# Three rows of a modulation matrix by DMA transpose and VectorE product-sums, and half of the row statistics on ScalarE

## The chip, the cores and the metric

The kernel runs on one core of a Trainium2 chip. The metric is the device time in microseconds (us) of one execution. Each kernel was executed several times, and the kernel before again beside each; a ratio is the mean time of one kernel's runs over that of the other's runs of the same rounds. The runs came in four jobs; each job had its own runs of the kernel before. The profile is one execution, whose span (first to last instruction) is about 2 us shorter than the reported time.

## The reference

```python
mod = (silu(c) @ w_mod).reshape(1, 6, 1, -1)         # c: 1 x 1024, w_mod: 1024 x 6144
sa, ca, ga, sb, cb, gb = ...                          # six rows of 1024
h = layernorm(x) * (1 + ca) + sa                      # x: 2048 x 1024
x = x + ga * linear_attention(h, wqkv) @ wo           # 32 heads of 32, phi(t) = elu-like
h = layernorm(x) * (1 + cb) + sb
x = x + gb * (silu(h @ w_gate) * (h @ w_up)) @ w_down # width 3584
```

Nearly all work is dense matmuls. The six rows of `mod` are 0.02% of its operations, but the kernel makes them in pieces on TensorE and VectorE, and this is what the change is about. `sa` and `ca` are needed at once and stay as they are; `ga`, `cb`, `sb` ("late rows") are needed from 129 us on, `gb` from about 380 us on.

## The kernel before

Tokens go in four chunks of 512 (four tiles of 128). A stage multiplies a chunk by one weight: K, V and Q stages have eight groups of eight matmuls, 128x128 by 128x512, into one PSUM bank; five banks rotate. The program issues each engine's instructions in a fixed order; `put(label, f)` places `f` behind the group of that label. So ("V", 1, 3) is the fourth V group of chunk 1. The late rows were made in two ways.

CB on TensorE, as one-column matmuls:

```python
def late_vec(q, kb, slot):                    # twice, 32 matmuls each
    for ii in range(NB // P):
        for j in range(DC):
            nc.tensor.matmul(bank[7][:, col:col + 1], lhsT=wml[slot][:, j, ii * P:(ii + 1) * P],
                             rhs=scT[:, j:j + 1], start=False, stop=(j == DC - 1), ...)
```

GA, SB (and GB) as partial sums on VectorE, eight multiply-adds for each half row, split into a high and a low bf16 part, and summed over the partitions by TensorE, either with an all-ones stationary operand (which also copies the row into all partitions) or into columns:

```python
def late_sum(acc, kb, slot, js):
    for j in js:                              # first one a plain multiplication
        nc.vector.scalar_tensor_tensor(out=dst, in0=wml[slot][:, j, :], scalar=scF[:, j:j + 1], in1=dst, ...)
def late_bc(kb, hl, dst):                     # GA and GB: 2 matmuls of 512 columns for a half row
    for s_ in range(2):
        nc.tensor.matmul(b[:], lhsT=ones[:], rhs=hl[:, s_, :], ...)
def late_cols(q, kb, hl):                     # SB: 8 one-column matmuls for a half row
    ...
```

Row statistics of the normalization (`ln_stats`: two `bn_stats`, one `bn_aggr`, on VectorE) feed GpSimd, which writes the normalized tile, and a DMA transpose on the SP queue puts it into place. A later VectorE instruction modulates it; the K stage of that chunk needs it.

## Time and profile before

| | kernel before |
|---|---|
| time, median of the first 4 runs | 842.47 us (842.31 to 842.87) |
| span of the profiled execution | 840.4 us |
| TensorE waits in it | 3.7 us, all before 27 us |
| VectorE busy in the V stages of chunks 1, 2, 3 | 13.3, 12.9, 13.5 of 14 us |
| TensorE time of the late rows GA, CB, SB | 2.89 us |

The lines behind this stand in the prediction. In the page, a digit of a slice row is the busy share of one fortieth of the span in tenths. In a timeline line the first two numbers are start and duration; TensorE's matmuls overlap (the eight transposes at 7.69 us last 0.62, and the next group starts at 8.15), so what a group costs is the distance to the next group's start.

### The profile page before, as it was taken

The page shows a single profiled execution, that of the slowest core. Times are in us where ns is not written, and L with a number is a line of the kernel's source. Part 1 is how long each engine was busy: PE and PEld are TensorE (multiplying, and loading weights), DVE is VectorE, ACT ScalarE, POOL GpSimd, SP SyncE. Part 2 cuts the span into 40 slices and gives each one's busy share as a digit, 9 for nine tenths or more (in the row PEclk, how much of TensorE's full clock was granted, in tenths as well). Part 3 has the DMA queues.
Part 4 walks back from the last instruction along what each step waited for, and adds up shares of the span by engine and source line. Part 5 has one row for each costly group of instructions (what it writes and reads, how often), then busy time and mean ns, then how long its engine had stood idle before and what let it go on. Part 6 is the DMA issues. An engine that isn't in the chain of part 4 may idle for free.

```text
span 840.4 us, 10723 instructions
## 1 busy us (share of the span) xinstructions
PE 833.5 (99%) x4292; PEld 391.3 (47%) x4292; DVE 356.5 (42%) x668; ACT 145.1 (17%) x271; POOL 79.9 (10%) x143
## 2 busy tenths in 40 slices
PE   8999999999999999999999999999999999999998
PEld 4454444544444444444444444444444444444445
DVE  5768779988655656635341111111101211111111
ACT  4333333323211111111110001111000111100000
POOL 2124220022122323100000000000000000000000
PEclk9999999999999999999999999999999999999999
DMA  9985491056599899787874225555322555211210
GB/s 291 310 244 138 133 243 46 16 154 133 126 225 225 224 226 287 190 248 226 251 241 142 76 69 151 151 151 152 105 75 82 156 155 152 76 38 44 76 69 26
DMA packets 203905, 128.62 MB, mean 153 GB/s; under 512 B 50768, under 2 KB 190032, under 8 KB 203856
## 3 DMA queue, kind: packets, MB, share of 16 engines
q1 hardware_dynamic: 163008, 98.58, 41.1%
q10 hardware_dynamic: 38544, 20.98, 11.4%
q0 software_dynamic: 2304, 8.39, 2.6%
q8 instruction: 33, 0.54, 0.3%
q14 instruction: 16, 0.13, 0.1%
HBM read 103.81 MB, written 12.58 MB: 139 GB/s over the span
## 4 chain that ended last, share of the span: by engine, by line
PE 97%; SPq 1%; DMA 1%; issue 0%; DVE 0%
PE bank L553 23%; PE bank L534 23%; PE bank L528 23%; PE bank L272 7%; PE bank L485 7%; PE bank L264 7%; PE bank L249 6%; DMA M<-in_w_mod_dram 1%; PE bank L458 1%; PE bank L281 1%; SPq L148 1%; SPq L145 0%; PE bank L342 0%; SPq L140 0%; PE bank L328 0%; PE bank L364 0%
## 5 line engine op out<-in xcount | busy, mean ns | idle before, releaser
L534 PE MATMUL bank<-M,M 128*128 128x512 bf16 x896 | 211.7, 379 | 0.0
L528 PE MATMUL bank<-M,M 128*128 128x512 bf16 x896 | 211.6, 379 | 0.0
L536 DVE TENSOR_TENSOR M<-bank,e 128x512 bf16<-128x512 f32 x112 | 77.5, 692 | 248.5 <-PE bank L534 247.1
L553 PE MATMUL bank<-M,M 128*128 128x512 bf16 (+2 forms) x728 | 148.0, 363 | 0.0
L531 ACT ACTIVATE e<-bank 128x512 f32<-128x512 f32 x112 | 66.8, 597 | 436.3 <-PE bank L528 423.6
L553 PEld LDWEIGHTS <-M 128*128 128x128 bf16 x952 | 90.9, 98 | 103.0
L534 PEld LDWEIGHTS <-M 128*128 128x128 bf16 x896 | 87.7, 98 | 105.7
L528 PEld LDWEIGHTS <-M 128*128 128x128 bf16 x896 | 87.3, 98 | 103.9
L556 DVE TENSOR_TENSOR M<-bank,M 128x512 bf16<-128x512 f32 (+2 forms) x34 | 22.5, 661 | 169.9 <-PE bank L553 169.9
L249 PE MATMUL bank<-M,M 128*128 128x512 bf16 x256 | 57.9, 379 | 1.0 <-DVE M L231 0.6
L485 PE MATMUL bank<-M,M 128*128 128x512 bf16 x256 | 57.9, 379 | 0.0
L272 PE MATMUL bank<-M,M 128*128 128x512 bf16 x256 | 57.7, 379 | 0.0
L264 PE MATMUL bank<-M,M 128*128 128x512 bf16 x256 | 55.9, 379 | 0.0
L244 ACT ACTIVATE e<-bank 128x512 f32<-128x512 f32 x64 | 37.8, 598 | 100.5 <-PE bank L272 48.8
L553 PE MATMUL bank<-M 128*128 128x512 bf16 x224 | 51.0, 379 | 0.0
L246 DVE SCALAR_TENSOR_TENSOR M<-bank,e 128x512 bf16<-128x512 f32 x64 | 44.3, 692 | 3.9
L264 PEld LDWEIGHTS <-M 128*128 128x128 bf16 x256 | 25.0, 98 | 30.2
L485 PEld LDWEIGHTS <-M 128*128 128x128 bf16 x256 | 25.0, 98 | 29.7
L249 PEld LDWEIGHTS <-M 128*128 128x128 bf16 x256 | 24.2, 98 | 29.5 <-DVE M L231 2.1
L245 DVE TENSOR_SCALAR e<-e 128x512 f32<-128x512 f32 x64 | 27.7, 433 | 23.4 <-ACT e L244 23.4
L272 PEld LDWEIGHTS <-M 128*128 128x128 bf16 x256 | 24.5, 98 | 27.6
L487 DVE TENSOR_TENSOR M<-bank,M 128x512 f32<-128x512 f32 x32 | 22.0, 689 | 13.3 <-PE bank L485 13.1
(74 smaller groups left out, 362.4 us busy)
## 6 DMA issues: line engine op xcount, KB each, us to landing
M<-in_B_w_gate_dram SPq DMA_DIRECT2D x56, 512.0 KB, 3.9
M<-in_B_w_up_dram SPq DMA_DIRECT2D x56, 512.0 KB, 4.9
M<-in_w_mod_dram SPq DMA_DIRECT2D x8, 1024.0 KB, 8.7
x_scratch<-M POOLq DMA_DIRECT2D x16, 512.0 KB, 5.6
M<-x_scratch ACTq DMA_DIRECT2D x16, 512.0 KB, 3.4
M<-in_B_w_down_dram SPq DMA_DIRECT2D x6, 1024.0 KB, 7.9
M<-in_A_x_dram SPq DMA_DIRECT2D x16, 256.0 KB, 6.6
M<-in_w_mod_dram SPq DMA_DIRECT2D x8, 512.0 KB, 7.1
```

What stands on the lines that cost most here:

```text
L244: nc.scalar.activation(out=e[:], in_=acc, func=ACT.Exp)
L245: nc.vector.tensor_scalar(out=e[:], in0=e[:], scalar1=1.0, scalar2=PHI_EPS, op0=ALU.min, op1=ALU.add)
L246: nc.vector.scalar_tensor_tensor(out=dst, in0=acc, scalar=0.0, in1=e[:], op0=ALU.max, op1=ALU.add)
L249: nc.tensor.matmul(acc[:], lhsT=M4[:, sc_, cc, t * P:(t + 1) * P], rhs=wk[:, cc, h * NB:(h + 1) * NB], start=(cc == 0), stop=(cc == DC - 1))
L264: nc.tensor.matmul(acc[:], lhsT=M4[:, sc_, cc, t * P:(t + 1) * P], rhs=wv[:, cc, h * NB:(h + 1) * NB], start=(cc == 0), stop=(cc == DC - 1))
L272: nc.tensor.matmul(acc[:], lhsT=wq[:, cc, qc * P:(qc + 1) * P], rhs=M4[:, sc_, cc, :], start=(cc == 0), stop=(cc == DC - 1))
L485: nc.tensor.matmul(acc[:], lhsT=oTs[st % 3][:, cc, :], rhs=wo[:, cc, hs], start=(cc == 0), stop=(cc == DC - 1))
L528: nc.tensor.matmul(g_ps[:], lhsT=wg_blk[:, cc, fs], rhs=M4[:, sc_, cc, :], start=(cc == 0), stop=(cc == DC - 1))
L531: nc.scalar.activation(out=sg[:], in_=g_ps[:], func=ACT.Silu)
L534: nc.tensor.matmul(u_ps[:], lhsT=wu_blk[:, cc, fs], rhs=M4[:, sc_, cc, :], start=(cc == 0), stop=(cc == DC - 1))
L536: nc.vector.tensor_tensor(out=gus[sc_][:, f, :], in0=u_ps[:], in1=sg[:], op=ALU.mult)
L553: nc.tensor.matmul(y_ps[:, 0:w], lhsT=gus[sc_][:, f, t * P:(t + 1) * P], rhs=wd(f)[:, c0:c1], start=(f == 0), stop=(f == FC - 1))
```

## The change

The intent: take the late rows off TensorE, and even out VectorE. A DMA transpose brings w_mod into SBUF with the outputs on the partitions, so that one VectorE product-sum per group of 128 outputs, against silu(c) copied into all partitions, gives a column of the row at once. GA is then spread to all partitions by copying the column along the free axis and transposing it on TensorE. To make room on VectorE, the statistics of every second tile of chunks 2 and 3 go to ScalarE as two passes with an accumulator, sum and sum of squared differences.

```diff
+    def ln_stats_act(st):
+        nc.scalar.activation(out=xns[st % 6], in_=x_sb, func=ACT.Copy, accum_out=sm[:, 0:1])
+        nc.scalar.mul(out=nmean[:], in_=sm[:, 0:1], mul=-1.0 / D)
+        nc.scalar.activation(out=xns[st % 6], in_=x_sb, func=ACT.Square, bias=nmean[:], accum_out=sm[:, 1:2])
+        ...                                              # three small GpSimd instructions
     def ln(st):
-        ln_stats(st)
+        if st >= 2 * STC and st % 2:
+            ln_stats_act(st)
+        else:
+            ln_stats(st)
...
+    def load_late(q, i, js):
+        for j in js:
+            nc.sync.dma_start_transpose(out=rowT[i][:, j], in_=wm_v[:, j, q * D:(q + 1) * D])
+
+    def late_sum(q, i, bs):
+        for b in bs:
+            nc.vector.tensor_tensor_reduce(out=prod..., in0=rowT[i][:, :, b, :], in1=sc_bc..., scale=1.0, scalar=0.0,
+                                           op0=ALU.mult, op1=ALU.add, accum_out=colF[:, q, b:b + 1])
+
+    def spread(eng, col):
+        eng.tensor_copy(out=rep[:], in_=col.unsqueeze(2).to_broadcast([P, DC, P]))
+
+    def late_bc(dst):
+        for cc in range(DC):
+            nc.tensor.transpose(tp[:, cc, :], rep[:, cc, :], ident[:])
+        nc.scalar.copy(out=dst[:]..., in_=tp)
...
+    spread(nc.vector, scT[:])
+    put(("V", 0, 5), lambda: late_bc(sc_bc))
+    put_late(GA, 0, [("Q", 0, k) for k in range(8)], [("V", 1, k) for k in range(8)])    # loads, sums
+    put(("K", 2, 3), lambda: late_bc(ga_bc))
+    put_late(CB, 1, [("V", 1, k) for k in range(8)], [("V", 2, k) for k in range(8)])
+    put(("V", 2, 7), lambda: nc.sync.dma_start(out=wo, in_=wo_v))                        # was at ("K", 2, 3)
+    put_late(SB, 0, [("V", 2, k) for k in range(8)], [("V", 3, k) for k in range(8)])
```

Cut: late_vec, late_cols and the split of GA and SB go; GB keeps the old way under new names; the normalization of chunks 2 and 3 moves one to three groups ahead, and the scaling of `wo` two groups back.

More of the change, by code (lines that the diff above doesn't have):

```diff
@@ L107 @@
     pqT = view(M3, 0, [NSC, HG, SCW])
-    wml = [view(M3, 4096 * (1 + i), [DC, NB]) for i in range(3)]
     wd_hi = view(M3, 0, [14, D])
@@ L120 @@
     obs = [view(M6, 4096 + 1024 * i, [D]) for i in range(2)]
-    accA = view(M5, 8256, [D], F32)
-    hlA = [view(M5, 10304 + 1024 * i, [2, NB]) for i in range(2)]
+    rowT = [view(M3, 4096, [DC, DC, P]), view(M6, 0, [DC, DC, P])]
+    prod = view(M5, 8256, [D], F32)
+    wmg = [view(M3, 4096 * (1 + i), [DC, NB]) for i in range(2)]
     accG = view(M3, 12288, [D], F32)
@@ L181 @@
     ga_bc = const.tile([P, D], BF16, name="ga_bc")
-    gb_bc = const.tile([P, D], BF16, name="gb_bc")
+    gb_bc = ga_bc
     KVZ = const.tile([P, HG, KVW], BF16, name="KVZ")
+    rep = const.tile([P, DC, P], BF16, name="rep")
+    sc_bc = const.tile([P, D], BF16, name="sc_bc")
+    colF = const.tile([P, 6, DC], F32, name="colF")
     ones = const.tile([P, P], BF16, name="ones")
@@ L213, in ln_stats @@
         stat[st] = (rstd, nmr)
+    def ln_stats_act(st):
+        x_sb = xs[st % 6]
+        sm = small.tile([P, 2], F32, name="sm")
+        nc.scalar.activation(out=xns[st % 6], in_=x_sb, func=ACT.Copy, accum_out=sm[:, 0:1])
+        nmean = small.tile([P, 1], F32, name="nmean")
+        nc.scalar.mul(out=nmean[:], in_=sm[:, 0:1], mul=-1.0 / D)
+        nc.scalar.activation(out=xns[st % 6], in_=x_sb, func=ACT.Square, bias=nmean[:], accum_out=sm[:, 1:2])
+        veps = small.tile([P, 1], F32, name="veps")
+        nc.gpsimd.tensor_scalar(out=veps[:], in0=sm[:, 1:2], scalar1=1.0 / D, scalar2=LN_EPS,
+                                op0=ALU.mult, op1=ALU.add)
+        rstd = small.tile([P, 1], F32, name="rstd")
+        nc.gpsimd.tensor_tensor(out=rstd[:], in0=veps[:], in1=neg_half[:], op=ALU.pow)
+        nmr = small.tile([P, 1], F32, name="nmr")
+        nc.gpsimd.tensor_tensor(out=nmr[:], in0=nmean[:], in1=rstd[:], op=ALU.mult)
+        stat[st] = (rstd, nmr)
     def ln_xn(st, pool):
@@ L295 @@
     GA, SB, CB, GB = 2, 3, 4, 5
-    def load_late(q, kb, slot):
-        k0 = q * D + kb * NB
-        nc.sync.dma_start(out=wml[slot], in_=wm_v[:, :, k0:k0 + NB])
-    def late_sum(acc, kb, slot, js):
-        dst = acc[:, kb * NB:(kb + 1) * NB]
+    def load_late(q, i, js):
[3 more added lines that the diff above has]
+        for b in bs:
+            nc.vector.tensor_tensor_reduce(out=prod.rearrange("p (j k) -> p j k", j=DC), in0=rowT[i][:, :, b, :],
+                                           in1=sc_bc[:].rearrange("p (j k) -> p j k", j=DC), scale=1.0, scalar=0.0,
+                                           op0=ALU.mult, op1=ALU.add, accum_out=colF[:, q, b:b + 1])
@@ new lines, in late_fin @@
+    def late_fin(q):
+        if q == SB:
+            nc.vector.tensor_copy(out=sbT[:], in_=colF[:, q, :])
+        else:
+            nc.vector.tensor_copy(out=m1[:, q, :], in_=colF[:, q, :])
+            if q == CB:
+                nc.vector.tensor_scalar_add(out=cb1T[:], in0=m1[:, q, :], scalar1=1.0)
+            else:
+                spread(nc.vector, m1[:, q, :])
+    def spread(eng, col):
+        eng.tensor_copy(out=rep[:], in_=col.unsqueeze(2).to_broadcast([P, DC, P]))
+    def late_bc(dst):
+        tp = nextbank()[:].bitcast(BF16).rearrange("p (c s) -> p c s", c=DC)
+        for cc in range(DC):
+            nc.tensor.transpose(tp[:, cc, :], rep[:, cc, :], ident[:])
+        nc.scalar.copy(out=dst[:].rearrange("p (c s) -> p c s", c=DC), in_=tp)
@@ L303, in late_sum, with load_gb, part_sum @@
+    def load_gb(kb):
+        k0 = GB * D + kb * NB
+        nc.sync.dma_start(out=wmg[kb], in_=wm_v[:, :, k0:k0 + NB])
+    def part_sum(kb, js):
+        dst = accG[:, kb * NB:(kb + 1) * NB]
         for j in js:
             if j == 0:
-                nc.vector.tensor_scalar_mul(out=dst, in0=wml[slot][:, 0, :], scalar1=scF[:, 0:1])
+                nc.vector.tensor_scalar_mul(out=dst, in0=wmg[kb][:, 0, :], scalar1=scF[:, 0:1])
             else:
-                nc.vector.scalar_tensor_tensor(out=dst, in0=wml[slot][:, j, :], scalar=scF[:, j:j + 1], in1=dst,
+                nc.vector.scalar_tensor_tensor(out=dst, in0=wmg[kb][:, j, :], scalar=scF[:, j:j + 1], in1=dst,
@@ L308, in late_sum @@
                                          op0=ALU.mult, op1=ALU.add)
-    def late_split(acc, kb, hl):
-        src = acc[:, kb * NB:(kb + 1) * NB]
-        nc.vector.tensor_copy(out=hl[:, 0, :], in_=src)
-        nc.vector.tensor_tensor(out=hl[:, 1, :], in0=src, in1=hl[:, 0, :], op=ALU.subtract)
-    def late_cols(q, kb, hl):
-        o = 320 + 8 * q
-        for ii in range(NB // P):
-            col = o + kb * (NB // P) + ii
-            for s_ in range(2):
-                nc.tensor.matmul(bank[7][:, col:col + 1], lhsT=hl[:, s_, ii * P:(ii + 1) * P], rhs=ones[:, 0:1],
-                                 start=False, stop=(s_ == 1), skip_group_check=True)
@@ L323, in late_vec @@
-    def late_vec(q, kb, slot):
-        o = 320 + 8 * q
-        for ii in range(NB // P):
-            col = o + kb * (NB // P) + ii
-            for j in range(DC):
-                nc.tensor.matmul(bank[7][:, col:col + 1], lhsT=wml[slot][:, j, ii * P:(ii + 1) * P],
-                                 rhs=scT[:, j:j + 1], start=False, stop=(j == DC - 1), skip_group_check=True)
-    def late_fin(q):
-        mps = bank[7][:, 320 + 8 * q:328 + 8 * q]
-        if q == SB:
-            nc.vector.tensor_copy(out=sbT[:], in_=mps)
-        else:
-            nc.vector.tensor_copy(out=m1[:, q, :], in_=mps)
-            nc.vector.tensor_scalar_add(out=cb1T[:], in0=m1[:, q, :], scalar1=1.0)
@@ L339, in late_bc, with part_split, part_bc @@
-    def late_bc(kb, hl, dst):
+    def part_split(kb):
+        src = accG[:, kb * NB:(kb + 1) * NB]
+        nc.vector.tensor_copy(out=hlG[:, 0, :], in_=src)
+        nc.vector.tensor_tensor(out=hlG[:, 1, :], in0=src, in1=hlG[:, 0, :], op=ALU.subtract)
+    def part_bc(kb):
         b = nextbank()
         for s_ in range(2):
-            nc.tensor.matmul(b[:], lhsT=ones[:], rhs=hl[:, s_, :], start=(s_ == 0), stop=(s_ == 1))
-        nc.scalar.copy(out=dst[:, kb * NB:(kb + 1) * NB], in_=b[:])
+            nc.tensor.matmul(b[:], lhsT=ones[:], rhs=hlG[:, s_, :], start=(s_ == 0), stop=(s_ == 1))
+        nc.scalar.copy(out=gb_bc[:, kb * NB:(kb + 1) * NB], in_=b[:])
@@ L602 @@
     for sc in (2, 3):
-        put_ln(sc, [("K", sc - 1, 1), ("K", sc - 1, 3), ("K", sc - 1, 5), ("K", sc - 1, 7),
-                    ("V", sc - 1, 4), ("V", sc - 1, 6)])
+        put_ln(sc, [("K", sc - 1, 0), ("K", sc - 1, 1), ("K", sc - 1, 3), ("K", sc - 1, 4),
+                    ("V", sc - 1, 2), ("V", sc - 1, 3)])
     put(("V", 0, 7), lambda: [load_x(st) for st in range(8, 12)])
-    put(("V", 1, 7), lambda: [load_x(st) for st in range(12, 16)])
-    def sums(acc, kb, slot, labels):
-        for i, lab in enumerate(labels):
-            put(lab, lambda i=i: late_sum(acc, kb, slot, (2 * i, 2 * i + 1)))
@@ L613 @@
-    put(("V", 0, 6), lambda: load_late(CB, 0, 0), lambda: load_late(CB, 1, 1), lambda: load_late(GA, 0, 2))
-    put(("K", 1, 2), lambda: late_vec(CB, 0, 0), lambda: load_late(GA, 1, 0))
-    put(("K", 1, 6), lambda: late_vec(CB, 1, 1), lambda: load_late(SB, 0, 1))
-    put(("V", 1, 7), lambda: late_fin(CB))
-    sums(accA, 0, 2, [("V", 1, k) for k in range(4)])
-    put(("V", 1, 3), lambda: late_split(accA, 0, hlA[0]), lambda: load_late(SB, 1, 2))
-    put(("K", 2, 2), lambda: late_bc(0, hlA[0], ga_bc))
@@ L620 @@
-    put(("K", 2, 3), lambda: nc.sync.dma_start(out=wo, in_=wo_v))
-    sums(accA, 1, 0, [("V", 2, k) for k in range(4)])
-    put(("V", 2, 3), lambda: late_split(accA, 1, hlA[1]))
-    put(("K", 3, 0), lambda: late_bc(1, hlA[1], ga_bc))
-    for kb in range(2):
-        sums(accA, kb, 1 + kb, [("V", 3, 4 * kb + k) for k in range(4)])
-    put(("V", 3, 4), lambda: late_split(accA, 0, hlA[0]))
-    put(("KV", 3, 0), lambda: late_split(accA, 1, hlA[1]))
-    put(("Q", 1, 2), lambda: late_cols(SB, 0, hlA[0]), lambda: late_cols(SB, 1, hlA[1]), lambda: late_fin(SB))
@@ L629, with put_late @@
-    put(("GU", 0, 18), lambda: load_late(GB, 0, 0), lambda: load_late(GB, 1, 1))
+    put(("K", 1, 7), lambda: [load_x(st) for st in range(12, 16)])
+    put(("V", 0, 5), lambda: late_bc(sc_bc))
+    def put_late(q, i, loads, sums):
+        for k in range(DC):
+            put(loads[k], lambda k=k: load_late(q, i, (k,)))
+            put(sums[k], lambda k=k: late_sum(q, i, (k,)))
+        put(sums[-1], lambda: late_fin(q))
+    put_late(GA, 0, [("Q", 0, k) for k in range(8)], [("V", 1, k) for k in range(8)])
@@ L630 @@
+    put(("K", 2, 3), lambda: late_bc(ga_bc))
+    put_late(CB, 1, [("V", 1, k) for k in range(8)], [("V", 2, k) for k in range(8)])
+    put(("V", 2, 7), lambda: nc.sync.dma_start(out=wo, in_=wo_v))
+    put_late(SB, 0, [("V", 2, k) for k in range(8)], [("V", 3, k) for k in range(8)])
+    put(("GU", 0, 18), lambda: load_gb(0), lambda: load_gb(1))
     gb_at = [("GU", 0, f) for f in range(21, FC)] + [("GU", 1, f) for f in range(8)]
     for kb in range(2):
-        sums(accG, kb, kb, gb_at[5 * kb:5 * kb + 4])
@@ L633 @@
-        put(gb_at[5 * kb + 3], lambda kb=kb: late_split(accG, kb, hlG))
-        put(gb_at[5 * kb + 5], lambda kb=kb: late_bc(kb, hlG, gb_bc))
+        for k in range(4):
+            put(gb_at[5 * kb + k], lambda kb=kb, k=k: part_sum(kb, (2 * k, 2 * k + 1)))
+        put(gb_at[5 * kb + 3], lambda kb=kb: part_split(kb))
+        put(gb_at[5 * kb + 5], lambda kb=kb: part_bc(kb))
     for cc in range(DC):
-        put(("K", 3, 2 + cc) if cc < 6 else ("V", 3, cc - 6),
-            lambda cc=cc: nc.vector.tensor_tensor(out=wo[:, cc, :], in0=wo[:, cc, :], in1=ga_bc[:], op=ALU.mult))
+        put(("K", 3, 4 + cc) if cc < 4 else ("V", 3, cc - 4), lambda cc=cc: nc.vector.tensor_tensor(out=wo[:, cc, :], in0=wo[:, cc, :], in1=ga_bc[:],
+                                                               op=ALU.mult))
```

## The prediction

> **What bounds the kernel now.** I read four views of the kernel before, in this order: the page (busy shares, slices, chain), the waits of TensorE, the timeline of TensorE where the removed instructions stand, and the groups and windows of VectorE in the stage that the change rewrites.
>
> From the page:
>
> ```profile
> span 840.4 us, 10723 instructions
> ...
> PE 833.5 (99%) x4292; PEld 391.3 (47%) x4292; DVE 356.5 (42%) x668; ACT 145.1 (17%) x271; POOL 79.9 (10%) x143
> ...
> PE   8999999999999999999999999999999999999998
> ...
> DVE  5768779988655656635341111111101211111111
> ...
> PE 97%; SPq 1%; DMA 1%; issue 0%; DVE 0%
> ```
>
> TensorE is busy in every slice and is 97% of the chain that ended last. Busy time alone proves little for a pipelined engine, so I looked at its waits: 3.7 us in all, the last before 27 us. After that it runs without a gap for 813 us, so time is saved only by TensorE instructions taken out of this stream, and lost only if another engine makes it stop. VectorE is full (8 or 9 tenths) only between 63 and 190 us; that is where it could make it stop, and it is where the change works.
>
> The timeline of TensorE around what is removed (L328, L342, L320), and, from the start of the kernel, around eight transposes like those added (L349); columns are start and duration in us:
>
> ```profile
> 7.69 0.62 PE L349 MATMUL bank<-ident,M 128*128 128x128 bf16 x8
> 8.15 0.81 PE L194 MATMUL bank<-M 128*128 128x512 bf16 x3
> ...
> 65.72 0.94 PE L328 MATMUL bank<-scT,M 128*128 128x1 bf16 x32
> 66.53 7.07 PE L249 MATMUL bank<-M,M 128*128 128x512 bf16 x32
> ...
> 96.77 0.59 PE L342 MATMUL bank<-M,ones 128*128 128x512 bf16 x2
> 97.20 8.80 PE L249 MATMUL bank<-M,M 128*128 128x512 bf16 x40
> ...
> 156.51 0.54 PE L320 MATMUL bank<-ones,M 128*128 128x1 bf16 x16
> 156.92 1.89 PE L272 MATMUL bank<-M,M 128*128 128x512 bf16 x8
> ```
>
> Durations overlap the next instruction, so a group's price is the distance to the next start: 32 one-column matmuls 0.81 us (25 ns each), two of 512 columns 0.43 us (215 ns each), 16 one-column ones 0.41 us, eight transposes 0.46 us (57 ns each). The group table's 379 ns and 163 ns would mislead.
>
> Groups of VectorE by form (busy us, mean ns), and three windows, the stages that multiply V for chunks 1, 2, 3:
>
> ```profile
> L536 DVE TENSOR_TENSOR M<-bank,e 128x512 bf16<-128x512 f32 x112 | 77.5, 692 | 248.5 <-PE bank L534 247.1 <-ACT e L531 1.1
> L307 DVE SCALAR_TENSOR_TENSOR M<-M,scF,M 128x512 f32<-128x512 bf16 x28 | 22.7, 810 | 0.9
> L203 DVE BATCH_NORM_STATS2 stats<-M 128x6 f32<-128x512 bf16 x32 | 20.4, 680 | 2.4 <-DMA M<-in_A_x_dram 2.4
> L467 DVE TENSOR_TENSOR M<-bank,rd 128x256 bf16<-128x256 f32 x16 | 6.6, 415 | 0.0
> ```
>
> ```profile
> 76.00:90.00 14.00, 14.00 (x70) 6.42 (x68) 13.34 (x26) 4.70 (x8) 5.00 (x6) 1.00 0.78 193
> 106.00:120.00 14.00, 14.00 (x71) 6.49 (x70) 12.91 (x25) 4.80 (x9) 4.99 (x6) 1.00 0.94 236
> 136.00:150.00 14.00, 14.00 (x73) 6.58 (x72) 13.54 (x23) 4.83 (x9) 0.00 (x0) 1.00 0.00 0
> ```
>
> The columns are span, then busy TensorE, weight load, VectorE, ScalarE, GpSimd, then clock, DMA share, GB/s. VectorE works 12.9 to 13.5 of 14 us there, TensorE all of it: VectorE is a close second.
>
> [...] here, while the row transposes run alone around 43 us, the DMA rows show 195 to 223 GB/s at full busy share[...]. [...] L221, with two pointers, measures 1240.
>
> **The change part by part.**
>
> TensorE loses the 64 one-column matmuls of CB (2 x 0.81 = 1.62 us), the 16 of SB (0.41) and the four broadcast matmuls of GA (2 x 0.43 = 0.86): 2.89 us. It gains two broadcasts by transposes, of silu(c) and of GA, 2 x 0.46 = 0.92 us. Net 1.97 us less, all on the path. GB keeps its old way.
>
> VectorE, off the path. Removed: the sums of GA and SB, four halves of one scaling (0.48) and seven multiply-adds of 0.75 to 0.81, about 6.0 us each, 24 us; four splits of 0.43 + 0.69, 4.5 us; statistics of four tiles, each 2 x 0.68 + 0.21 + 0.15 = 1.7, 6.9 us. Sum 35.4. Added: 24 product-sums over 1024 elements. No such operation is in this trace; from the slope of tensor_tensor, (692 - 415)/256 = 1.08 ns an element, 1024 elements give 692 + 554 = 1.25 us, and with the read of the accumulator I take 1.3 as an estimate: 31.2 us. Two spreads of 128x1024, 0.7 to 1.2 each, and some small casts: 3 us. Sum 34. In total VectorE is even. By stage: V of chunk 1 gets 8 x 1.3 = 10.4 of sums, 3.3 of modulation (eight of 0.41) and 1.4 of finish, 15 us against its TensorE length of 13.8, but the K stage before it is lighter by two tiles of statistics (3.4 us), so the work starts earlier and K2's first matmul needs only the modulation, third in the queue. Chunk 2 has 13.9 us, chunk 3 has 10.4 + 2.7 of the scaling of wo = 13.1, less than the 15 us which the page's groups give it today.
>
> ScalarE gets two passes of about 1.2 us and a small multiply for four tiles, some 3 us each, 12 us in all, two per K stage. An exponential (0.60) behind them is late by under 3 us. A bank comes back after four further groups of 8 x 0.216 = 1.73 us, 6.9 us; emptying it takes 0.60 + 0.43 + 0.69 = 1.7. So some 5 us of lateness are free, and this one is hidden. Copy and Square may call for another activation table (1.28 us a load in the trace, and back); even that, 2.6 us more, barely reaches the 5.
>
> DMA: 24 transposes of 256 KB take the place of six loads of 1 MB, the same bytes. SBUF to SBUF they issue in 1.25 us and land in 3.2; at 210 GB/s each is 1.25 us of all engines, a row of eight 10 us. GA is issued near 52 us and needed near 78; CB near 80 and needed near 107; SB near 107 and needed near 137. All three are hidden. The load of wo (2 MB, 10.2 us to landing) now waits for CB's last sum, near 122 us, and is first needed after K group 4 of chunk 3, near 132: just in time, with VectorE perhaps 0 to 3 us late, within the 5 us.
>
> The spread of silu(c) in the prologue falls into a VectorE idle of 1.69 us ahead of 28.9 us: free.
>
> Sum: 842.5 - 2.0 = 840.5; I add 0.3 for small waits, 840.8.
>
> **The rivals.** First, the product-sum is slow. At 2 us instead of 1.3 each V stage would hold 16 + 3.3 us in 13.8; the backlog passes 5 us and TensorE loses perhaps 2 to 4 us in each of three stages: 845 to 852. For it: it is a fused operation with an fp32 output that no row of this trace has timed. [...]
>
> Second, transposes out of DRAM are slower than those between SBUF tiles[...], and the rows' own transposes stand behind them in the same queue. At 2.5 us each, SB ends near 128 and wo lands near 137, VectorE stands 5 us, TensorE 0 to 3: 841 to 844. At 5 us each, GA would land near 92 instead of 62, the modulation behind its sums would be late, and K2 and K3 would stall by 10 to 30 us: 855 to 870. Against: 3.2 us to landing for the same size here, and a lead of 25 us per row.
>
> Third, relief of VectorE buys something. It can't: after 27 us TensorE waits for nobody.
>
> **Range and chances.** Most of the weight is on the bare 2 us, down to 840.2 if nothing waits; the first rival and the mild second stretch it upwards only. A range of 839.5 to 846 should hold it 8 times in 10. Faster by 2% would need 17 us that TensorE does not have to give: 0.01. Slower by 2% needs a rival at its worst: 0.06. Within: 0.93.
>
> **What would show it.** Right: TensorE's count is 4292 - 84 + 16 = 4224, its waits still end before 28 us, both new groups of eight transposes cost 0.46 us, and stages lie earlier by 0.4 to 2 us. VectorE's busy time changes by under 5 us, a product-sum has about 1.3 us, ScalarE grows by some 13. Wrong: waits of TensorE for VectorE or a bank between 60 and 160 us; a product-sum over 1.6 us; VectorE waiting for the transposed row or for wo; landing of the late transposes far above 5 us. The prediction fails outright if such waits sum to more than 5 us.

Where a cut is marked, a passage was taken out. 842.5 less 2.0, plus 0.3, comes to 840.8, and the 2.0 rests on the start-to-start distances of TensorE above. Measured in the kernel before: 195 to 223 GB/s behind the 210 of the DMA estimate, and 1240 ns for a ScalarE pass over 1024 elements behind the estimate of about 1.2 us. The estimate of 0.7 to 1.2 us for a spread lies between a VectorE copy of 128x1024 in that trace (L357, 686 ns) and the 1.25 us that the slope of tensor_tensor gives.

## The result, and the profile after

The changed kernel took 841.25 us (median of 4 runs, 840.28 to 842.46) against 842.47 us; the ratio was 0.9986 with a 95% interval of 0.9968 to 1.0003: the same within 2%. The interval includes 1, so these four runs alone show no gain. The four runs were not one group: 842.11 and 842.46, 840.28 and 840.39. The profiled one was 842.11.

The page of the changed kernel, the lines that answer to those of before, and the new group of product-sums:

```profile
span 840.2 us, 10541 instructions
...
PE 827.6 (99%) x4144; PEld 389.8 (46%) x4224; DVE 354.4 (42%) x663; ACT 155.0 (18%) x291; POOL 78.9 (9%) x147
...
DVE  4668888788655656635341111111101211111111
...
PE 96%; SPq 1%; DMA 1%; issue 1%; DVE 0%; DVEq 0%
...
L325 DVE CUSTOM_DVE_ANT_0 M<-M,sc_bc 128x1024 f32<-128x1024 bf16 x24 | 29.8, 1241 | 0.5
```

The picture is the same: TensorE is the chain. The 4224 weight loads are the matmul count (80 matmul records are missing from this trace), 68 fewer than before. VectorE is busy for 2.1 us less, ScalarE for 9.9 us more.

The timeline of TensorE in this profile:

```profile
43.33 0.61 PE L345 MATMUL bank<-ident,rep 128*128 128x128 bf16 x8
43.77 3.62 PE L286 MATMUL bank<-M,M 128*128 128x512 bf16 x16
...
62.86 13.98 PE L271 MATMUL bank<-M,M 128*128 128x512 bf16 x63
76.67 13.98 PE L286 MATMUL bank<-M,M 128*128 128x512 bf16 x62
```

The transposes cost 0.44 us; the K stage of chunk 1 (L271) runs through, 13.81 us to the next start, where it took 15.42 with CB's columns in it. Yet it begins at 62.86 instead of 60.54 us, 2.32 later, of which the transposes explain 0.46. The other 1.86 us are lost in the prologue (all before the V stage of chunk 0, at 31 us), where the two kernels execute the same TensorE stream. The windows of that stretch (span; busy time of TensorE, weight load, VectorE, ScalarE, GpSimd with counts; then the granted TensorE clock, 1.00 at full speed, DMA share, GB/s), first of before, then of after:

```profile
20.00:22.00 2.00, 1.44 (x21) 0.72 (x21) 0.84 (x5) 0.00 (x0) 0.00 (x0) 1.00 1.17 305
22.00:24.00 2.00, 2.00 (x10) 0.94 (x11) 0.26 (x1) 0.00 (x0) 0.00 (x0) 1.00 1.17 307
```

```profile
20.00:22.00 2.00, 1.04 (x19) 0.71 (x20) 0.41 (x4) 0.00 (x0) 0.00 (x0) 1.00 1.17 308
22.00:24.00 2.00, 1.78 (x5) 0.60 (x5) 0.69 (x2) 0.00 (x0) 0.00 (x0) 0.51 1.17 304
```

A load of w_mod came 0.4 us later, and then the clock was granted at half for some 3.5 us (0.51 at 22 to 24 us, 0.64 at 24 to 26): 18 matmuls took 5.57 us instead of 4.07. The saving of the change was there, and this execution paid it back by something else. Whether the change causes the dip was open, and is what the first experiments ask. A second profile of the same kernel (e1 below) had no dip. The lines of the K stage of chunk 1 and of what follows it, first of before, then of e1, where the last wait of TensorE is that of the first line:

```profile
60.54 5.34 PE L249 MATMUL bank<-M,M 128*128 128x512 bf16 x24
...
75.96 13.98 PE L264 MATMUL bank<-M,M 128*128 128x512 bf16 x64
```

```profile
26.39 4.91 PE L271 MATMUL bank<-M,M 128*128 128x512 bf16 x21 [0.34 <-DVE saT L396]
...
61.02 13.98 PE L271 MATMUL bank<-M,M 128*128 128x512 bf16 x63
74.83 13.98 PE L286 MATMUL bank<-M,M 128*128 128x512 bf16 x62
```

The starts of the stages in us:

| start of | before | after, first profile | after, e1 | e1 minus before | by the prediction's steps |
|---|---|---|---|---|---|
| V of chunk 0 | 31.10 | 32.97 | 31.13 | +0.03 | 0 |
| K of chunk 1 | 60.54 | 62.86 | 61.02 | +0.48 | +0.46 |
| V of chunk 1 | 75.96 | 76.67 | 74.83 | -1.13 | -1.16 |
| V of chunk 2 | 105.83 | 106.56 | 104.72 | -1.11 | -1.13 |
| V of chunk 3 | 135.71 | 136.00 | 134.16 | -1.55 | -1.56 |
| first attention readout | 158.64 | 158.54 | 156.70 | -1.94 | -1.97 |
| end of the span | 840.4 | 840.2 | 838.5 | -1.9 | -1.97 |

### The profile page after: what moved, and what is told of

Same layout as the page of the kernel before. It is cut to its first block, busy times and chain, and to the rows that moved or that the text cites. A ratio compares the mean times of both kernels' runs of the same rounds, so it can differ in the third digit from the quotient of the medians.

```text
span 840.2 us, 10541 instructions
## 1 busy us (share of the span) xinstructions
PE 827.6 (99%) x4144; PEld 389.8 (46%) x4224; DVE 354.4 (42%) x663; ACT 155.0 (18%) x291; POOL 78.9 (9%) x147
## 4 chain that ended last, share of the span: by engine, by line
PE 96%; SPq 1%; DMA 1%; issue 1%; DVE 0%; DVEq 0%
PE bank L562 23%; PE bank L581 23%; PE bank L556 23%; PE bank L513 7%; PE bank L286 7%; PE bank L294 7%; PE bank L271 6%; DMA M<-in_w_mod_dram 1%; PE bank L486 1%; PE bank L303 1%; SPq L148 1%; SPq L145 0%; SPq L140 0%; PE bank L391 0%; PE bank L345 0%
## 5 line engine op out<-in xcount | busy, mean ns | idle before, releaser
L271 PE MATMUL bank<-M,M 128*128 128x512 bf16 x247 | 58.1, 386 | 1.6 <-DVE M L253 0.6
L267 DVE TENSOR_SCALAR e<-e 128x512 f32<-128x512 f32 x64 | 29.4, 460 | 23.0 <-ACT e L266 23.0
L271 PEld LDWEIGHTS <-M 128*128 128x128 bf16 x256 | 24.7, 99 | 30.8 <-issue 2.3
L325 DVE CUSTOM_DVE_ANT_0 M<-M,sc_bc 128x1024 f32<-128x1024 bf16 x24 | 29.8, 1241 | 0.5
```

The costliest lines, as they stand in the source:

```text
L271: nc.tensor.matmul(acc[:], lhsT=M4[:, sc_, cc, t * P:(t + 1) * P], rhs=wk[:, cc, h * NB:(h + 1) * NB], start=(cc == 0), stop=(cc == DC - 1))
L325: nc.vector.tensor_tensor_reduce(out=prod.rearrange("p (j k) -> p j k", j=DC), in0=rowT[i][:, :, b, :], in1=sc_bc[:].rearrange("p (j k) -> ...
```

## The experiments

Theory P: only TensorE's stream sets the time; the change takes 1.97 us out of it, all its other work is hidden, and a dip of the clock in the prologue, which comes by chance to both kernels, adds some 2 us to some executions. Rivals: Q, the change costs what it saves through waits; R, the change provokes the dip; S, it is the relief of VectorE that matters.

**e1: the changed kernel again.** No edit.

> The changed kernel again, unaltered, to see its scatter. Theory P (only TensorE's stream counts): executions fall into two groups, one near 840.3 us and one near 842.2; the upper group is a half-speed stretch of the TensorE clock in the prologue (0.51 at 22 to 24 us in the first profile), 1.5 us, plus some 0.4 us of a late load there, and it comes by chance. Then the kernel before, in the same rounds, should now and then show such an execution too, near 844.3, and otherwise 842.4. Rival Q (the change itself costs what it saves, through waits of TensorE for another engine after 28 us): all executions near 842 and no low group, with waits after 28 us in the profile. Rival R (the change provokes the dip): the upper group appears in the changed kernel only.

Measured: 840.64 us (840.37 to 841.03, 6 runs), ratio 0.9971 (0.9958 to 0.9984). No execution of the upper group came, and the profile has no TensorE wait after 27 us: Q falls. The kernel before, on the same chip, had 844.48, 844.70 and 844.77 among 11 runs, with mean clocks of 0.997 and 0.998: R falls too. Over all jobs the kernel before had 10 of 35 runs from 844.13 up, mean 844.49, and 25 from 842.11 to 842.98, mean 842.44; in the ten runs the changed kernel had in all, eight had a mean of 840.56. Low group against low group the change is worth 1.88 us, 0.22% (1.81 us within e1's job). This also explains the two ratios: in the first job two of four changed runs were high and none of before, in this one it was the other way round.

The half clock itself was seen in the profiles of the changed kernel (above), of e6 and of e7. No profile of the kernel before fell on a high run. There it is argued from the same 2 us and from the mean clock: 0.996 to 0.998 in all ten high runs, 0.999 or 1.0 in all but two of the 21 low ones of the three later jobs.

**e2: the changed kernel with all statistics on VectorE.**

```diff
-        if st >= 2 * STC and st % 2:
-            ln_stats_act(st)
-        else:
-            ln_stats(st)
+        ln_stats(st)
```

> The changed kernel with all row statistics on VectorE as before, so the transposed rows and product-sums alone. VectorE gets 6.9 us more work in the K stages of chunks 1 and 2. Theory P: the same as the changed kernel, 840.3 without the clock dip, 842.2 with it, because the lateness stays under the some 5 us that the five banks give. Rival S (moving the statistics is what makes the change work): 1 to 4 us slower than the changed kernel of the same state, with TensorE waiting between 76 and 130 us.

Measured: 841.10 us (840.66 to 842.94, 6 runs; two of them high), ratio 0.9982. The profile's span is 838.2 us against e1's 838.5, and TensorE's last wait ends before 28 us. By the spans (mean 838.5 us in the four low runs, 838.6 in e1's six) the transposed rows alone give the whole saving. By the reported time they don't quite: the four low runs have a mean of 840.97, 0.3 above e1's. The reported time lies about 0.4 us further above the span than in e1 (2.4 against 2.0 us), outside what the profile shows; why is open. One of the two high runs, 842.94, had a mean clock of 1.0, so not every high run is shown to be a clock dip.

**e3: the kernel before with nothing but the statistics moved.**

```diff
-        ln_stats(st)
+        if st >= 2 * STC and st % 2:
+            ln_stats_act(st)
+        else:
+            ln_stats(st)
```

> The kernel before with nothing but the statistics of the odd tiles of chunks 2 and 3 moved to two ScalarE passes. Theory P: 842.4, the same as before to 0.2 us, because TensorE executes the same stream and waited for nobody. Rival S: 1 to 3 us faster, since VectorE sheds 6.9 us in its fullest stretch.

Measured: 842.52 us (842.14 to 844.75, 6 runs), ratio 0.9997. VectorE has 4.5 us less busy time and nothing follows. S, which asked for 1 to 4 us in e2 and 1 to 3 us here, falls on both sides: moving the statistics alone gains nothing, and the saving comes without it but for the open 0.3 us of e2.

**e4: the changed kernel with filler in the prologue's gaps.**

```diff
+    def fill(n):
+        for _ in range(n):
+            nc.tensor.matmul(bank[7][:, 128:512], lhsT=zt[:, 0:P], rhs=zt[:, 0:384], start=True, stop=True)
     def mod_pair(p):
         mod_mm(0, 2 * p, 2 * p + 2)
+        if p == 2: fill(5)
         mod_mm(1, 2 * p, 2 * p + 2)
+        if p == 2: fill(2)
```

> The changed kernel with seven 384-column matmuls on zeros in the prologue's two gaps around 20 to 22 us (five ahead of the second half of the third early group, two behind it), about 1.1 us of TensorE work where it stood waiting. Theory P with the clock explanation: no execution with the half-speed stretch, so all executions near 840.4 (839.9 to 840.9). If the dip is set by something else than idling there, the two groups of the changed kernel remain, 840.5 and 842.4.

Measured: 840.92 us, all five runs between 840.84 and 841.04. No dip, and less scatter, but e1 had none in six runs either, so this alone shows little.

**e4b: the same filler in the kernel before.** Same edit.

> The kernel before with the same seven filler matmuls in the prologue. The first job refuted rival R: the kernel before had 3 of 11 executions at 844.5 to 844.8, with a granted clock of 0.997 or 0.998. If idling in the two gaps is what lowers the clock, this kernel has no execution above 843.5 and lies at 842.6 to 842.9 (the filler costs about 0.2 to 0.4 us where the load comes early); the plain kernel before, in the same rounds, again shows some near 844.6. If the dip has another cause, some executions here lie near 844.8 too.

Measured: 842.66 us (842.35 to 842.92, 5 runs); in the same rounds the plain kernel before had four of 11 from 844.13 up. With e4 and e11 the filled prologue had no run 2 us up in 15 (e10 can't be counted, its clock falls elsewhere); at the plain kernel's rate of 10 in 35 that has a chance of (25/35)^15, under 1%. So in these runs the dip came only without the filler, which left TensorE 0.2 us of waiting for the load of w_mod in e4 and none in e4b; what brings it on was not shown. Nor did it come with every longer wait. In the profiles of the changed kernel, of e6 and of e7 TensorE waited 1.1 to 1.2 us for that load of w_mod, and the clock fell (0.50 to 0.58 at 22 to 24 us); in those of e3 and e8 it waited as long, and the clock stayed at 1.00. In the five with a wait of 0.3 to 0.8 us (before, e1, e2, e5, e9) it stayed, too. The windows of e3, to be held against those of the changed kernel above:

```profile
20.00:22.00 2.00, 1.01 (x19) 0.71 (x20) 0.39 (x4) 0.00 (x0) 0.00 (x0) 1.00 1.17 303
22.00:24.00 2.00, 1.92 (x9) 0.73 (x9) 0.71 (x2) 0.00 (x0) 0.00 (x0) 1.00 1.14 303
```

What decides between the two outcomes is open. The filler costs some 0.2 to 0.4 us in the runs that would not have dipped. In the changed kernel it gains nothing on average (e4's mean is 840.93, that of the ten plain changed runs 840.90); in the kernel before the filled mean is 842.62 against 843.02 of the 35 plain runs.

**e5: the price of one-column matmuls, tenfold.**

```diff
+    put(("K", 1, 2), ... lambda: idle_vec(0, 9)); the same at ("K", 1, 6)   # late_vec's loop nine times, into columns 400 to 403
```

> The kernel before with CB's 64 one-column matmuls followed by nine more such sets into unused columns of the bank, 576 more instructions. Theory P, a price of 0.81 us per 32: 9 x 1.62 = 14.6 us more, 857.1 (856.5 to 857.8; 2 us more in an execution with the clock dip). If the price on the path were what the group table shows as the mean, 163 ns each, it would be 94 us more; if such matmuls hid beside the weight loads, nothing.

Measured: 862.24 us (862.00 and 862.48): a miss by 5 us. The added stretches take 7.54 and 7.70 us, 15.2 in all and close to the 14.6 expected. The rest is clock. Windows of it:

```profile
70.00:72.00 2.00, 2.00 (x81) 2.00 (x79) 0.00 (x0) 0.00 (x0) 0.20 (x1) 0.50 0.44 63
...
76.00:78.00 2.00, 2.00 (x6) 0.69 (x5) 0.00 (x0) 0.27 (x1) 0.00 (x0) 0.50 0.99 345
```

TensorE is busy for the whole of both windows, with 81 one-column matmuls in the first, and the granted clock is 0.50 in both (it was 1.00 at 66 to 68 us and 0.68 at 68 to 70); the ordinary matmuls behind pay (six in 2 us instead of eleven). So in this run the clock fell without a wait of TensorE; why was not shown. In the kernel before, 32 of them in 0.81 us amid dense matmuls left it at 1.00 (64 to 68 and 72 to 76 us). In the prologue 32 stand in the same 2 us as a wait for a load; whether they have a part in the dip there, no run tested apart.

**e6: twenty more broadcasts by transposes.**

```diff
-    put(("V", 0, 5), lambda: late_bc(sc_bc))
+    put(("V", 0, 5), lambda: late_bc(sc_bc), lambda: idle_bc(20))   # late_bc's eight transposes, no copy
```

> The changed kernel with 20 more broadcasts by eight transposes each, unused, in the V stage of chunk 0: the price of what the change adds to TensorE, taken twenty times. Theory P: 20 x 0.456 = 9.1 us more, 849.6 (849.2 to 850.2). The row of one-column matmuls taken tenfold brought 15.2 us of its own and some 4 us of half clock behind it[...].

The cut clause named the dearer case, 851 to 853 us.

Measured: 849.40 us; the runs without the prologue's dip 849.15 to 849.59, so 8.6 to 9.0 us more for 20, 0.43 to 0.45 each. The profiled run, 851.17, had the dip in the prologue (0.50 at 22 to 24 us), and none behind 160 transposes. The first two lines are their timeline (9.15 us to the next start, 0.457 for eight), the third is a window amid them:

```profile
43.89 9.10 PE L352 MATMUL bank<-ident,rep 128*128 128x128 bf16 x160
53.04 3.40 PE L286 MATMUL bank<-M,M 128*128 128x512 bf16 x15
...
48.00:50.00 2.00, 2.00 (x40) 2.00 (x38) 0.00 (x0) 0.00 (x0) 1.70 (x3) 1.00 0.85 168
```

The granted clock was 1.00 amid these transposes of 128 columns (44 to 52 us), where it was 0.50 amid e5's one-column matmuls. The price of what the change adds is as counted.

**e7: each product-sum twice.**

```diff
-            put(sums[k], lambda k=k: late_sum(q, i, (k,)))
+            put(sums[k], lambda k=k: late_sum(q, i, (k, k)))
```

> The changed kernel with each of the 24 product-sums done twice, 30 us more of VectorE between 79 and 150 us (1.24 us each). Theory P says VectorE is the close second: the extra 10.4 us per V stage exceed the some 5 us that the banks give, so TensorE stalls 3 to 10 us in each of K2, K3 and Q1, together 12 to 22 us: 852 to 863. It also sizes my first rival (a product-sum of 2 us instead of 1.3). Rival Q' (there is more room than I counted): below 845.

Measured: 863.32 us (862.13 to 864.03, 4 runs), 0.3 above the stated range. TensorE's longest waits, with their total, number and longest:

```profile
PE bank L486 <- DVE KVZ L313: 7.4, 1, 7.4
PE bank L345 <- DVE rep L340: 4.0, 1, 4.0
PE bank L271 <- DVE M L268: 4.0, 2, 3.5
```

That is 15.4 us. The other 8 us of the profiled run (863.95, against 840.56) are clock: it had the dip in the prologue (0.58 and 0.57 at 22 to 26 us, some 1.7 us), and half clock behind these waits (0.50 at 105 to 107, 143 to 145 and 174 to 182 us). One stall was not where I had put it: chunk 2's K stage stopped for GA's spread, ahead of the broadcast's transposes, not for a bank. VectorE is indeed the close second, and by estimate from this run a product-sum of 2 us would have cost several us.

**e8: the load of wo held back.**

```diff
-    put(("V", 2, 7), lambda: nc.sync.dma_start(out=wo, in_=wo_v))
+    put(("K", 3, 4), lambda: nc.vector.memset(wo[:, :, 0:2], 0.0), lambda: nc.sync.dma_start(out=wo, in_=wo_v))
```

> The changed kernel with the load of wo held back until VectorE has done the fifth K group of chunk 3, right ahead of its first use. VectorE then stands for about 9 us. Theory P, with some 5 us of free lateness from the five banks: TensorE stops once, about 4 us, in the V stage of chunk 3[...]: 844 to 847. If the free lateness were much larger than I counted, 840.5; if TensorE followed VectorE directly, 850.

The range of 844 to 847 holds a term of 1.5 to 2 us; without it 840.5 and about 4 make 844.5.

The small memset is there so that the load must wait for VectorE. Measured: 845.36 us (844.62 to 847.42, 4 runs). The first line is TensorE's wait, the second a window behind it:

```profile
PE bank L286 <- DVE M L268: 4.0, 1, 4.0
```

```profile
142.00:144.00 2.00, 2.00 (x5) 0.64 (x5) 1.90 (x4) 0.00 (x0) 0.00 (x0) 0.50 1.20 291
```

VectorE stood for 8.8 us and TensorE for 4.0: the free lateness is 4.8 us, as counted from the banks. The run whose clock stayed at 1.0 took 844.62, which is 840.6 and the wait; the profiled one lost 2.7 us more in the 48 matmuls behind it (0.50 at 142 to 146 us, 0.65 at 146 to 148). There the wait of 4.0 us cost 6.7.

**e9: the transposes one stage later.**

```diff
-    put_late(GA, 0, [("Q", 0, k) for k in range(8)], ...     # CB at ("V", 1, k), SB at ("V", 2, k)
+    put_late(GA, 0, [("K", 1, k) for k in range(8)], ...     # CB at ("K", 2, k), SB at ("K", 3, k)
```

> The changed kernel with each row's eight transposes issued one stage of eight groups later (GA with K1, CB with K2, SB with K3), so that they stand in the queue between and behind the transposes of the normalized rows and the lead to their use is cut to about 10 us. Theory P: the sums of GA start near 90 us instead of 79, those of CB near 130 instead of 108, the modulation that stands behind the first two sums is late, and TensorE waits about 5 us ahead of K2 and 9 ahead of K3[...]: 853 to 864. If the lead was far more than is needed: 840.5 to 842.

The range of 853 to 864 holds a term of some 3 us; without it 840.5, 5 and 9 make 854.5.

Measured: 864.11 us (863.53 to 864.74, 4 runs), 0.1 above the stated range. VectorE waited for the rows 32.5 us in three waits, and TensorE 10.1 us for the modulation (0.6 of it in the prologue, as always), which stands behind the first sums in VectorE's order:

```profile
PE bank L271 <- DVE M L253: 10.1, 5, 5.0
```

Ahead of K2 these waits were 5.0 and 0.55 us, ahead of K3 3.8 and 0.55, where 9 had been expected. What the expectation lacked is a wait of 3.5 us for KVZ ahead of the first readout and one of 1.0 us for a bank. Waits behind the prologue thus sum to 14 us of the 23.5 more than 840.6; the rest goes with half clock behind them (0.50 at 95 to 101, 133 to 138 and 178 to 182 us). So the lead is needed: the change is right to load a row a stage and more ahead, before the queue fills with the transposes of normalized tiles.

**e10: GB the same way, with the filler.**

```diff
-    put(("GU", 0, 18), lambda: load_gb(0), lambda: load_gb(1))
-    ...                                                       # partial sums, split, ones-matmuls
+    put(("GU", 0, 27), lambda: load_late(GB, 0, range(DC)))   # eight transposes at once
+    ...                                                       # eight late_sum at ("GU", 1, 3) to ("GU", 1, 6), late_bc at ("GU", 1, 7)
```

> The changed kernel taken further: the last row, GB, goes the same way (DMA transposes, product-sums, broadcast by eight transposes) and the filler is in. Theory P: TensorE loses four more 512-column matmuls, 2 x 0.43 us, and gains 0.46, so 0.4 us less than the filled changed kernel's 840.9: 840.5 (840.1 to 840.9), no execution near 842. Its VectorE work lies where VectorE is a fifth busy, so no waits are expected. Rival: the transposes from memory disturb the loads of the gate and up weights at the end of the first chunk and TensorE waits there, 841 to 844.

Measured: 846.41 us (845.77 to 848.17, 6 runs): a miss, and the stated rival came, costlier than its 841 to 844. The SP queue at that place:

```profile
352.16 10.85 SPq L321 DMA_TRANSPOSE M<-in_w_mod_dram  x8
363.11 0.53 SPq L552 DMA_DIRECT2D M<-in_B_w_gate_dram  x1
```

Eight transposes held the queue for 10.85 us, the gate weights of the next group were issued only after them, TensorE waited 3.4 us for those and then ran at half clock (0.50 at 368 to 372 us).

**e11: GB's transposes one per group.** As e10, but the transposes stand at ("GU", 0, 27) and ("GU", 1, 0) to ("GU", 1, 6), the sums at ("GU", 1, 9) to ("GU", 1, 12), the broadcast at ("GU", 1, 13), the scaling of w_down behind it.

> The row GB by transposes again, now one transpose per group of the second chunk's gate and up stage instead of eight at once, with the sums, the broadcast and the scaling of the down weights moved behind it, and the filler in. In the burst version TensorE waited 3.4 us for a gate load that stood behind ten us of transposes in the same issuing queue. If that queueing was the cause, the wait is gone and Theory P's arithmetic holds: 0.4 us below the filled changed kernel's 840.9, so 840.5 (840.2 to 840.9). If transposes from memory disturb the weight loads in themselves (bandwidth), waits remain: 842 to 846.

Measured: 841.18 us (841.03 to 841.76, 5 runs), 0.3 above the stated range. The wait for gate weights is gone, as the queueing explains. The transfers were slower there, too, which e11 doesn't separate: the two gate loads behind e10's transposes took 6.4 us to landing (median), against 3.9 in the kernel before. But issued 10 us earlier they would by estimate from these figures have come in time even so. What remains is a wait of TensorE for the spread ahead of GB's transposes:

```profile
400.16 0.62 PE L345 MATMUL bank<-ident,rep 128*128 128x128 bf16 x8 [0.74 <-DVE rep L340]
```

This 0.74 us is more than the 0.4 us saved; against e4's 840.92 the run is 0.26 us worse. With the broadcast one group later it should give the 0.4 us; that version was not run. No version tried beats the changed kernel clearly.

## Why the prediction was right

It said 840.8 us, 839.5 to 846, and "within 2%"; the job measured 841.25. That this lies so near is luck: no run took 841.25, it is the middle of two low and two high ones. What bears the prediction out is 840.56, the mean of the eight low runs, against its bare 840.5, and the steps below.

- TensorE's stream: every step of the 2.89 - 0.92 = 1.97 us is in the table of stage starts within 0.03 us, and the low groups differ by 1.88. e6 priced the added part; e5 priced the removed kind at 26 to 27 ns instead of 25, most of it at half clock.
- VectorE: the estimate of 1.3 us for a product-sum measured 1.24 + 0.08 us for the accumulator's read, 1.27 from start to start (one took 1.7). The spreads took 0.69 us each, the lower end of my 0.7 to 1.2. In total VectorE was even (-2.1 us), and it never made TensorE stop. The prediction read the slices loosely: two of those between 63 and 190 us have 7 tenths, not 8 or 9.
- ScalarE grew by 9.9 us, not some 13. The passes took 1.05 and 1.15 us, each with 0.19 for the accumulator's read, and no table load was added (three in both profiles).
- DMA: a late transpose landed in 4.3 us (median), slower than the 3.2 taken from SBUF to SBUF, as the second rival held; each took 1.3 us to issue (median), a row of eight some 11 to 12 us, where 10 was taken. wo landed in 8.7 us and VectorE did not wait for it, where I had allowed 0 to 3 us.
- The 5 us of free lateness: 4.8 in e8.
- The rivals: neither came in the changed kernel, and both came when forced: e7 shows the first at double length (15.4 us of TensorE waits), e9 the lead of the second (14 us).

What the prediction lacked is the prologue's clock dip. It gave 0.3 us to "small waits"; it should have given the time two groups, 2 us apart, with about a quarter of the runs in the upper one, as large a term as the change itself. The four runs of before, all low, gave no hint of it.

## What to carry to other kernels

When one engine is 97% of the chain and never waits, price a change by the start-to-start distances of what it takes out of that engine's stream; relief of another engine was worth nothing here (e3), but their lateness is free only up to a bound that can be counted (here five banks, 4.8 us). In e8's profiled run a TensorE wait of 4.0 us cost 6.7, with the granted clock at 0.50 behind it, and in three profiles here a wait of 1.1 to 1.2 us in the prologue was followed by 0.50 to 0.58, in two others it was not: look at the granted clock of each run before a difference of 0.2% is believed. And the DMA transposes held the queue that issued them for over a microsecond each (10.85 us for eight in e10), so when loads that are needed soon use the same queue, put the transposes between them one at a time.
